# A fused polysketch attention and squared-ReLU layer: weights kept as loaded, one-run queries, padded tail keys, squares on GpSimd

## The chip, the cores and the metric

The kernel runs on one core of one Trainium2 chip. Its time is device time in microseconds (us) of one execution. The instructions belong to five engines: TensorE (PE in the profile, with its weight loads as PEld), VectorE (DVE), ScalarE (ACT), GpSimd (POOL) and SyncE (SP), which only issues transfers here. Each engine works through its own instructions in the order in which the program holds them; between engines, semaphores make one wait for another. A profile is one execution on the chip as the hardware recorded it.

## The reference

Inputs are `q`, `k`, `v` of 4 batches, 4 heads, 1088 tokens and 32 elements, two sketches `S1` and `S2` of 8x32, and the weights of a feed-forward layer. All are float32.

```python
def phi(x):                                   # 32 -> 64 features
    a = np.einsum('rd,bhsd->bhsr', S1, x)
    b = np.einsum('rd,bhsd->bhsr', S2, x)
    return np.einsum('bhsi,bhsj->bhsij', a, b).reshape(*x.shape[:-1], r * r)
q_p, k_p = (phi(q), phi(k))
kv = np.einsum('bhsf,bhsd->bhfd', k_p, v)
z = np.sum(k_p, axis=2)
num = np.einsum('bhsf,bhfd->bhsd', q_p, kv)
den = np.einsum('bhsf,bhf->bhs', q_p, z)[..., None] + 1e-06
x = (num / den)                               # -> 4352 tokens x 128
h = x @ w_in                                  # w_in 128 x 2048
g = np.maximum(h, 0.0) ** 2
out = g @ w_out                               # w_out 2048 x 128
```

## The kernel before

The attention is done batch by batch in float32. For the keys of a batch, `keys` turns `k` with 32x32 transposes on DVE (`kT`), multiplies by the sketches on PE (`kpr`, line 484), turns the result into `kab` (line 496), and forms the outer products `kp` (line 118, on POOL for most). 1088 tokens over 128 partitions give 8 full columns `l` = 0 to 7 and a ninth, `l` = 8, that fills only 64 partitions. `gram` (`z`, line 350) sums products of the sketched keys for the denominator, and `kvsum` (`kv`, line 365) multiplies `kp` by `v`; both have 64-partition matmuls for the ninth column. `kv_out` copies the sum out (`KVT`), turns it (`rep`) and copies it again (`KVr`).

For the queries of a batch, `queries` turns `q`, multiplies it by sketch and denominator weights, and brings that into `ab`. Batch 0 has a path of its own. Batch 1 does it with eight matmuls in two pieces (line 708) that ACT copies out. Batches 2 and 3 use small 32x32 tiles of the PE array: two pieces, each with eight matmuls for two of the four heads (line 728), and each transposed into `ab` by DVE (line 736). Then come the division (`tm`, `dn`, `rc`, `am`), the outer product `qp`, its transpose `tp`, and the multiplication by `KVr` (`x`, lines 592 and 622), whose result is copied out as bf16 (`xe`).

The feed-forward layer, `chunk`, takes 512 tokens at a time in eight chunks, and a ninth of 256 tokens (chunk 8, the tail tokens of all batches). A chunk has groups of 1024 columns of hidden values. `f1` (line 803) makes them in two PSUM banks with two matmuls of 512 columns, `re` is the ReLU out of PSUM (on ACT, line 812, or DVE, line 814), `sq` the square (on DVE, line 819, or ACT, line 821), and `f2` (line 827) multiplies by `w_out` with eight matmuls of 128 columns. `r` and `g` have four buffers each, the hidden values two pairs of banks for most groups. `oe` copies a chunk's output out of PSUM and `st` stores it.

`w_in` is cast to bf16 by `cast_w` (`cwi`) in four parts. In memory a part's hidden columns lie as `c`, `u` with `u` = 0 to 3 the fastest; the cast reads them with a step of four and writes each `u` together.

What runs when isn't decided at run time: `define` only records operations, and the string `ORDER` lists them by name, with `@ENGINE` where an operation can run on several. The instructions of each engine follow that list. Operations named `wm` are matmuls on zeros that fill PE's time in the first part. `BANKS` gives the PSUM bank of each value. The numbers beside an operation in `define` (such as `0.432`) were used to make the list and do nothing in the kernel.

Of the kernel before, what the change touches and what calls it, by code (L numbers as in the profile page):

```python
# [10 lines left out]
F32 = mybir.dt.float32  # L11
# [28 lines left out]
FILLS = 46  # L40


def define(W, tc, sb, ps, q, k, v, S1, S2, moe_w_in, moe_w_out, out):
# [12 lines left out]
    v_rest = sb.tile([64, B, H, D], F32, name="v_rest")  # L56
# [24 lines left out]
    w_in_b = sb.tile([128, CT, 128], BF16, name="w_in_b")  # L81
# [198 lines left out]
    def cast_w(i):  # L280
        @op("ACT", f"cwi{i}", act(512), r=[f"w_in_f{i}"], w=[f"w_in{i}"], alt=[("DVE", dve(512), 0)])
        def _(e):
            copy(
                e, w_in_b[:, 4 * i : 4 * i + 4], w_in_f[:, 512 * i : 512 * (i + 1)].rearrange("p (c u) -> p u c", u=4))

    def cast_wo(i):
        @op("ACT", f"cwo{i}", act(512), r=[f"w_out_f{i}"], w=[f"w_out{i}"], alt=[("DVE", dve(512), 0)])
        def _(e):
            copy(e, w_out_b[:, 4 * i : 4 * i + 4], w_out_f[:, 4 * i : 4 * i + 4])
# [51 lines left out]
    def gram(b, part):  # L341
# [4 lines left out]
        @op("PE", f"z{b}_{part}", 0.06 if part == 0 else 0.31, r=[f"kab{i}_{l}" for l in ls], w=[f"z{b}"], ps=[f"KZ{b}"])  # L346
        def _():
            for l in ls:
                x, pp = l % 4, 128 if l < NL else 64
                nc.tensor.matmul(  # L350
                    bank(f"KZ{b}")[32 * x : 32 * x + 32, 64:96],
                    kab[i][:pp, 1, l].rearrange("p h r -> p (h r)"), kab[i][:pp, 0, l].rearrange("p h r -> p (h r)"),
                    start=(l < 4), stop=(l + 4 > NL), skip_group_check=True)

    def kvsum(b, l0, n, last):
        i = b % 2
        r = [f"kp{i}_{l}" for l in range(l0, l0 + n)]
        r += [f"v_in{b}c{c}" for c in range(4)] if l0 < NL else [f"v_rest{b}"]

        @op("PE", f"kv{b}_{l0}", 0.10 * n, r=r, w=[f"kvt{b}"], ps=[f"KZ{b}"], after=[f"z{b}_0"])  # L360
        def _():
            for l in range(l0, l0 + n):
                pp = 128 if l < NL else 64
                for h in range(H):
# [3 lines left out]
                        kp[i][:pp, l, h].rearrange("p x y -> p (x y)"),  # L368
# [89 lines left out]
    def keys(b):  # L458
# [12 lines left out]
        else:  # L471
            spans = [(0, 4), (4, 4)] if b == 0 else [(0, 8)]
            for l0, n in spans:
# [3 lines left out]
                @op("PE", f"kpr{b}_{l0}", 0.28 if n == 4 else 0.63,  # L477
# [101 lines left out]
    def x_of(b, nm, l0, n, src, tn, pr, kind, rest=False):  # L579
# [4 lines left out]
        for f in range(2):  # L584
            @op("PE", f"{val}_{f}", 0.14 if n == 4 else 0.16, ps=[val],
# [25 lines left out]
    def x_whole(b, src, tn):  # L611
# [5 lines left out]
        @op("PE", f"x{b}", 1.43, ps=vals, r=[f"{tn}_{l}" for l in range(NL)] + [f"KVr{b}"], w=vals)  # L617
# [77 lines left out]
    def queries(b):  # L695
# [22 lines left out]
        else:  # L718
            for pr in range(2):
                val = f"qq{b}_{pr}"  # L720
                W.value(val, 2, "m")

                @op("PE", f"qpr{b}_{pr}", 0.59, r=[f"qT{i}_0", f"qT{i}_1", "Wqc", "Wqpad", f"Wqz{b}"], w=[val], ps=[val])
                def _(pr=pr, val=val):
                    for c in range(4):
                        for e in range(2):
                            h = 2 * pr + e
                            nc.tensor.matmul(  # L728
                                bank(val, e)[32 * c : 32 * c + 32, :256],
                                Wq[32 * h : 32 * h + 32, b].rearrange("p a r -> p (a r)"),  # L730
                                qT[i][32 * h : 32 * h + 32, :, c, :], start=True, stop=True, skip_group_check=True)
# [49 lines left out]
    def chunk(ci):  # L781
        rest = ci == 8
        ng = 4 if rest else 8
        W.value(f"o{ci}", 1, "o")
# [7 lines left out]
        nu = 1024 // N  # L792
        for g in range(ng):
            n = sum(8 for _ in range(ci)) + g
            hv = f"h{ci}_{g}"
            W.value(hv, 2, "h")

            @op("PE", f"f1_{ci}_{g}", 0.432, r=xk + [f"w_in{(nu * g + nu - 1) // 4}"], w=[hv], ps=[hv])
            def _(g=g, hv=hv):
                p0 = W.bank_of[hv]  # L800
                hh = P[:, p0 : p0 + 2].rearrange("p b n -> p (b n)")
                for u in range(nu):
                    nc.tensor.matmul(  # L803
# [204 lines left out]
```

## Time and profile before

| | |
|---|---|
| time, median of 3 runs | 107.2 us (106.2 to 108.21) |
| time of the profiled execution | 106.24 us |
| its span | 104.5 us |
| PE busy | 97.6 us, 93% of the span |
| DVE busy | 88.3 us, 85% |
| ACT busy | 87.4 us, 84% |
| POOL busy | 36.8 us, 35% |

The span is the part of the execution that the profile covers; 1.74 us of the profiled time lie around it. The profiled execution is at the fast end of the runs shown. The lines of one engine overlap a little at their ends, so that a run of eight instructions lasts less than eight times one of them; where the prediction needs the pace of an operation, it takes it from such a run.

### The profile page before, as it was taken

What the parts mean: (1) busy time and instruction counts of PE and PEld (TensorE: products, weight loads), DVE (VectorE), ACT (ScalarE), POOL (GpSimd) and SP (SyncE); (2) the same over time, 40 slices, a digit from 0 to 9 for tenths busy, and PEclk for the clock granted to TensorE, in tenths of its full rate; (3) what the DMA queues carried; (4) which work ended last, traced back from release to release, by engine and by line L of the source; (5) the groups of instructions that cost most, each with busy time, mean ns of one, the idle gap of its engine ahead of it and who ended that gap; (6) DMA issues with size and microseconds to landing.
All of it is one profiled execution on the core that took longest, in us unless ns stands there. A gap on an engine that the chain in (4) does not pass through costs nothing.

```text
span 104.5 us, 4039 instructions
## 1 busy us (share of the span) xinstructions
PE 97.6 (93%) x1716; PEld 68.1 (65%) x1716; DVE 88.3 (85%) x169; ACT 87.4 (84%) x105; POOL 36.8 (35%) x58
## 2 busy tenths in 40 slices
PE   5979999899899999999999999999999999999930
PEld 4757785377766665476777647677857677669930
DVE  2076898699799999999999999999998799999800
ACT  3104856999999999999999999999978999998910
POOL 3039436394049890026999700900000000000000
PEclk9999999999999999999999999999999999999996
DMA  2999999999998000000000300232000002510341
GB/s 80 340 252 309 296 281 396 316 202 242 292 189 171 30 9 0 6 0 0 0 9 10 122 0 6 69 86 102 0 6 0 0 0 60 137 38 9 98 112 42
DMA packets 7911, 11.28 MB, mean 108 GB/s; under 512 B 2261, under 2 KB 4949, under 8 KB 7893
## 3 DMA queue, kind: packets, MB, share of 16 engines
q1 hardware_dynamic: 7764, 10.98, 39.5%
q8 instruction: 13, 0.21, 1.0%
q10 hardware_dynamic: 128, 0.04, 0.2%
q14 instruction: 6, 0.04, 0.1%
HBM read 8.79 MB, written 2.23 MB: 105 GB/s over the span
## 4 chain that ended last, share of the span: by engine, by line
PE 83%; ACT 6%; DMA 4%; issue 2%; DVE 1%
PE P L827 30%; PE P L803 28%; PE P L365 5%; DMA k_in<-in_k_dram 4%; PE P L622 4%; ACT r L812 4%; PE P L728 2%; PE P L592 2%; PE P L196 2%; PE P L665 2%; PE P L484 2%; PE P L350 1%; PE P L381 1%; ACT w_in_b L115 1%; PE P L708 1%
## 5 line engine op out<-in xcount | busy, mean ns | idle before, releaser
L812 ACT ACTIVATE r<-P 128x1024 bf16<-128x1024 f32 x59 | 57.2, 1061 | 1.7 <-PE P L803 0.7
L827 PEld LDWEIGHTS <-g 128*128 128x128 bf16 x544 | 34.1, 98 | 11.7 <-ACT g L821 0.8
L827 PE MATMUL P<-w_out_b,g 128*128 128x128 bf16 x544 | 39.3, 219 | 0.0
L803 PE MATMUL P<-xT,w_in_b 128*128 128x512 bf16 x128 | 37.3, 379 | 0.6 <-ACT r L812 0.6
L819 DVE TENSOR_TENSOR g<-r 128x1024 bf16<-128x1024 bf16 x47 | 30.7, 682 | 2.5 <-PE P L827 1.4
L821 ACT ACTIVATE g<-r 128x1024 bf16<-128x1024 bf16 x21 | 21.8, 1108 | 0.0
L118 POOL TENSOR_TENSOR kp<-kab 128x512 f32<-128x512 f32 (+2 forms) x19 | 16.8, 907 | 2.0 <-DVE kab L496 2.0
L803 PEld LDWEIGHTS <-w_in_b 128*128 128x128 bf16 x144 | 11.8, 99 | 4.8 <-issue 2.8
L118 POOL TENSOR_TENSOR qp<-ab 128x512 f32<-128x512 f32 (+1 forms) x14 | 13.0, 945 | 1.8 <-DVE ab L118 1.5
L814 DVE TENSOR_SCALAR r<-P 128x1024 bf16<-128x1024 f32 x9 | 10.6, 1211 | 0.3 <-ACT r L812 0.2
L575 DVE STREAM_TRANSPOSE qpT<-qp 128x1024 f32<-128x1024 f32 (+2 forms) x12 | 10.1, 862 | 0.1
L196 PE MATMUL P<-zeros 128*128 128x256 bf16 x46 | 7.7, 313 | 1.1 <-DVE zeros L193 1.1
L297 DVE STREAM_TRANSPOSE kT<-k_in 128x512 f32<-128x512 f32 x8 | 5.3, 677 | 3.3 <-DMA k_in<-in_k_dram 3.3
L118 POOL TENSOR_TENSOR ab<-ab,rec 128x256 f32<-128x256 f32 (+1 forms) x4 | 2.3, 572 | 11.9 <-DVE rec L546 11.9
L196 PEld LDWEIGHTS <-zeros 128*128 128x128 bf16 x46 | 4.6, 112 | 2.8 <-DVE zeros L193 1.0
L118 POOL TENSOR_TENSOR tmp<-ab 128x256 f32<-128x256 f32 x2 | 1.8, 923 | 9.7 <-DVE ab L736 5.5
L365 PE MATMUL P<-kp,v_in 128*32 128x64 f32 x256 | 4.8, 221 | 0.0
L365 PEld LDWEIGHTS P<-kp,v_in 128*32 128x32 f32 x256 | 3.8, 110 | 1.4 <-issue 0.6
L115 DVE COPY osb<-P 128x512 f32<-128x512 f32 x7 | 4.7, 670 | 0.0
L622 PE MATMUL P<-qpT,KVr 32*32 32x256 f32 x192 | 4.5, 385 | 0.0
L496 DVE STREAM_TRANSPOSE kab<-P 128x512 f32<-128x512 f32 (+1 forms) x5 | 2.8, 583 | 1.9 <-PE P L484 1.9
L297 DVE STREAM_TRANSPOSE qT<-q_in 128x512 f32<-128x512 f32 x6 | 4.1, 682 | 0.0
(91 smaller groups left out, 87.8 us busy)
## 6 DMA issues: line engine op xcount, KB each, us to landing
k_in<-in_k_dram SPq DMA_DIRECT2D x4, 544.0 KB, 6.0
v_in<-in_v_dram SPq DMA_DIRECT2D x16, 128.0 KB, 6.4
q_in<-in_q_dram SPq DMA_DIRECT2D x3, 544.0 KB, 7.7
out_dram<-osb SPq DMA_DIRECT2D x24, 64.0 KB, 1.7
w_in_f<-in_moe_w_in_dram SPq DMA_DIRECT2D x4, 256.0 KB, 5.9
w_out_f<-in_moe_w_out_dram SPq DMA_DIRECT2D x4, 256.0 KB, 6.2
q_in<-in_q_dram SPq DMA_DIRECT2D x1, 512.0 KB, 6.0
out_dram<-osb SPq DMA_DIRECT2D x2, 256.0 KB, 3.4
```

The lines of the kernel that those rows point to most:

```text
L118: (nc.gpsimd if e == "POOL" else nc.vector).tensor_tensor(op=ALU.mult, **kw)
L196: W.op("PE", name, 0.107, lambda: nc.tensor.matmul(P[:, 3, :256], zeros[:, :128], zeros, start=True, stop=True, skip_group_check=True), r= ...
L297: nc.vector.transpose(dst[:, l0 : l0 + 4], src[:, :32].rearrange("p (c l) d -> p l c d", c=4)[:, l0 : l0 + 4])
L365: nc.tensor.matmul(bank(f"KZ{b}")[32 * h : 32 * h + 32, 0:64], v_in[b][:, h, l, :] if l < NL else v_rest[:, b, h, :], kp[i][:pp, l, h].rea ...
L575: nc.vector.transpose(dst[:, l0 : l0 + n].rearrange("p l h f t -> p (l h f t)"), src[:, l0 : l0 + n].rearrange("p l h x y -> p (l h x y)"))
L622: nc.tensor.matmul(bank(vals[c // 2], c % 2)[32 * h : 32 * h + 32, :256], KVr[b][32 * c : 32 * c + 32, f, 32 * h : 32 * h + 32], src[32 * ...
L803: nc.tensor.matmul(hh[:, N * u : N * (u + 1)], w_in_b[:, nu * g + u, :], x(), start=True, stop=True, skip_group_check=True)
L812: nc.scalar.activation(rt[n % NR], h, ACTF.Relu)
L814: nc.vector.tensor_scalar_max(rt[n % NR], h, 0.0)
L819: nc.vector.tensor_mul(gt[n % NG], rt[n % NR], rt[n % NR])
L821: nc.scalar.activation(gt[n % NG], rt[n % NR], ACTF.Square)
L827: nc.tensor.matmul(bank(f"o{ci}")[:, 128 * m : 128 * m + 128], gt[n % NG][:, N * u + 128 * m : N * u + 128 * m + 128], w_out_b[:, nu * g + ...
```

## The change

Parts of the code:

- `w_in_b` keeps the order of memory. The cast reads and writes without a step, and the weight load of `f1` reads 128 columns with a step of four elements.
- The queries of batch 1 go the way of batches 2 and 3. For these three batches one piece `qpr` of 16 matmuls for all four heads takes the place of two of eight, and DVE transposes its two halves into `ab`. `Wq` and its padding are as before.
- The ninth column of the keys is padded to 128 partitions: `pads` writes zeros once, and `gram` and `kvsum` use 128 partitions for all nine.
- A square may run on POOL.
- In chunk 8 the last group of 1024 columns becomes two groups of 512, each with one bank. Its output lies in two banks, copied out by ACT and DVE at once. Two of the four stores of chunk 7 are issued by ACT's queue.
- There are six fills fewer, and a new list `ORDER` with new `BANKS`. ReLUs: 59 on ACT and 9 on DVE before, 50 and 19 now. Squares: 21 on ACT and 47 on DVE before, 24 and 35 now, and 10 on POOL. `kv` is split into more separate pieces between the feed-forward matmuls: for batches 1, 2 and 3 it was 3, 1 and 1 pieces, and is 5, 3 and 2.

```diff
-    v_rest = sb.tile([64, B, H, D], F32, name="v_rest")
+    v_rest = sb.tile([128, B, H, D], F32, name="v_rest")
...
-    w_in_b = sb.tile([128, CT, 128], BF16, name="w_in_b")
+    w_in_b = sb.tile([128, 4, 128, 4], BF16, name="w_in_b")
...
+    @op("DVE", "pads", 1.1, w=["pads"])
+    def _():
+        nc.vector.memset(v_rest[64:], 0.0)
+        for i in range(2):
+            nc.vector.memset(kab[i][64:, :, NL], 0.0)
+            nc.vector.memset(kp[i][64:, NL], 0.0)
...
         def _(e):
-            copy(
-                e, w_in_b[:, 4 * i : 4 * i + 4], w_in_f[:, 512 * i : 512 * (i + 1)].rearrange("p (c u) -> p u c", u=4))
+            copy(e, w_in_b[:, i].rearrange("p c u -> p (c u)"), w_in_f[:, 512 * i : 512 * (i + 1)])
...
             for l in ls:
-                x, pp = l % 4, 128 if l < NL else 64
+                x = l % 4
                 nc.tensor.matmul(
                     bank(f"KZ{b}")[32 * x : 32 * x + 32, 64:96],
-                    kab[i][:pp, 1, l].rearrange("p h r -> p (h r)"), kab[i][:pp, 0, l].rearrange("p h r -> p (h r)"),
+                    kab[i][:, 1, l].rearrange("p h r -> p (h r)"), kab[i][:, 0, l].rearrange("p h r -> p (h r)"),
...
                         v_in[b][:, h, l, :] if l < NL else v_rest[:, b, h, :],
-                        kp[i][:pp, l, h].rearrange("p x y -> p (x y)"),
+                        kp[i][:, l, h].rearrange("p x y -> p (x y)"),
...
+            if b in QW:
+                vals = [f"qq{b}_{pr}" for pr in range(2)]
...
+                @op("PE", f"qpr{b}", 0.57, r=[f"qT{i}_0", f"qT{i}_1", "Wqc", "Wqpad", f"Wqz{b}"], w=vals, ps=vals)
+                def _(vals=vals):
+                    for c in range(4):
+                        for h in range(H):
+                            nc.tensor.matmul(
+                                bank(vals[h // 2], h % 2)[32 * c : 32 * c + 32, :256],
+                                Wq[32 * h : 32 * h + 32, b].rearrange("p a r -> p (a r)"),
+                                qT[i][32 * h : 32 * h + 32, :, c, :], start=True, stop=True, skip_group_check=True)
...
+        groups = [(0, 4), (4, 4), (8, 4), (12, 2), (14, 2)] if rest else [(2 * g, 2) for g in range(8)]
+        for g, (u0, nu) in enumerate(groups):
...
                     nc.tensor.matmul(
-                        hh[:, N * u : N * (u + 1)], w_in_b[:, nu * g + u, :], x(), start=True, stop=True,
+                        hidden()[:, N * u : N * (u + 1)], w_in_b[:, v // 4, :, v % 4], x(), start=True, stop=True,
...
-                if e == "DVE":
-                    nc.vector.tensor_mul(gt[n % NG], rt[n % NR], rt[n % NR])
+                r_, g_ = rt[n % NR][:, :cols], gt[n % NG][:, :cols]
+                if e != "ACT":
+                    product(e, out=g_, in0=r_, in1=r_)
...
+        if rest:
+            for m, e0 in enumerate(("ACT", "DVE")):
+                @op(e0, f"oe_{ci}{m}", act(128) if m == 0 else dve(128), r=[ov[m]], w=[f"osb{oi}_{m}"], ps=[ov[m]])
+                def _(m=m, e0=e0):
+                    copy(e0, osb[oi][:, m], o_of(m))
...
+                eng = "ACT" if ci == 7 and c > 1 else "SP"
...
-    TMK, TMQ, XW = (), (1,), (1, 2, 3)
+    TMK, TMQ, XW, QW = (), (), (1, 2, 3), (1, 2, 3)
...
-kp1_0@POOL kp1_6@POOL kp1_2@POOL kp1_4@POOL kp1_8@POOL f1_0_3 re_0_3@DVE x04_1_0 x04_0_0 x04_0_1
+tp0qp06 kab1_0 re_0_1@ACT sq_0_0@POOL kp1_8@POOL Wqc f1_0_2 f1_0_3 x04_1_0 x04_1_1 z1_0 z1_1
```

Three places show what the new list does. The first is POOL, from the end of batch 0 to the queries of batch 1. The tile `kp1` holds the key products of batch 1, `kp0` those of batches 0 and 2; `g0` to `g3` and `r0` to `r3` are the buffers of the feed-forward layer. Before:

```order
L118 TENSOR_TENSOR qp0_90<-ab0_87 128x256 x2
L252 TENSOR_TENSOR Wqf_145<-STS_136,maskh_139 128x4x16
L118 TENSOR_TENSOR kp1_86<-kab1_84 128x512 x4
L118 TENSOR_TENSOR kp1_86<-kab1_84 64x256
L118 TENSOR_TENSOR tmp1_97<-ab1_88 128x32x8
L118 TENSOR_TENSOR ab1_88<-ab1_88,rec1_103 128x32x8
L118 TENSOR_TENSOR qp1_91<-ab1_88 128x512 x4
```

The same place of the changed kernel:

```order
L118 TENSOR_TENSOR qp0_90<-ab0_87 128x256 x2
L118 TENSOR_TENSOR g0_124<-r0_120 128x1024
L118 TENSOR_TENSOR kp1_86<-kab1_84 64x256
L266 COPY Wq_144<-STS_136 128x4x16
L118 TENSOR_TENSOR kp1_86<-kab1_84 128x512 x4
L118 TENSOR_TENSOR g0_124<-r0_120 128x1024
L118 TENSOR_TENSOR g3_127<-r3_123 128x1024
L118 TENSOR_TENSOR ab1_88<-ab1_88,rec1_103 128x32x8
L118 TENSOR_TENSOR qp1_91<-ab1_88 128x512 x2
```

Three squares (`sq_0_0`, `sq_0_4`, `sq_0_7`) now stand around the key products of batch 1, and a product of the division (`tmp1`) has gone to DVE.

The second is DVE in chunk 0. `r` written from `P` is a ReLU, `g` from `r` a square, `qT1` and `kT0` are turned inputs of batches 1 and 2. Before:

```order
L819 TENSOR_TENSOR g2_126<-r2_122 128x1024
L819 TENSOR_TENSOR g3_127<-r3_123 128x1024
L425 TENSOR_REDUCE Wq_144<-P_63 128x8
L115 CAST w_out_b_134<-w_out_f_132 128x512
L819 TENSOR_TENSOR g0_124<-r0_120 128x1024
L819 TENSOR_TENSOR g1_125<-r1_121 128x1024
L819 TENSOR_TENSOR g2_126<-r2_122 128x1024
```

The changed kernel, in the same chunk:

```order
L848 TENSOR_SCALAR r3_123<-P_63 128x1024
L118 TENSOR_TENSOR g1_125<-r1_121 128x1024
L398 TENSOR_TENSOR Gm1_112<-P_63,maskg_141 128x32
L848 TENSOR_SCALAR r0_120<-P_63 128x1024
L848 TENSOR_SCALAR r1_121<-P_63 128x1024
L303 STREAM_TRANSPOSE qT1_81<-q_in1_69 128x512
L431 TENSOR_REDUCE Wq_144<-P_63 128x8
L303 STREAM_TRANSPOSE qT1_81<-q_in1_69 128x512
L848 TENSOR_SCALAR r3_123<-P_63 128x1024
L757 STREAM_TRANSPOSE ab1_88<-P_63 128x2x8x32 x2
```

In chunk 0 DVE has mostly ReLUs now and a single square, and the two transposes of batch 1's queries, which ACT copied before.

The third is the end of ACT's list; `osb1` is the output of chunk 7, `osb2` that of chunk 8. Before:

```order
L812 ACTIVATE r2_122<-P_63 128x1024
L812 ACTIVATE r3_123<-P_63 128x1024
L115 COPY osb1_129<-P_63 128x512
L115 COPY osb2_130<-P_63 128x256
L844 DMA out_0_dram<-osb2_130 32x256
```

The end of ACT's list in the changed kernel:

```order
L846 ACTIVATE r2_122<-P_63 128x1024
L846 ACTIVATE r3_123<-P_63 128x512
L115 COPY osb1_129<-P_63 128x512
L902 DMA out_0_dram<-osb1_129 32x512 x2
L115 COPY osb2_130<-P_63 128x128
L887 DMA out_0_dram<-osb2_130 32x256
```

The last ReLU and the last copy are half as wide, and two stores of chunk 7 are issued between the two copies.

More of the change, by code (lines that the diff above doesn't have):

```diff
@@ L357, in kvsum @@
         r = [f"kp{i}_{l}" for l in range(l0, l0 + n)]
-        r += [f"v_in{b}c{c}" for c in range(4)] if l0 < NL else [f"v_rest{b}"]
-        @op("PE", f"kv{b}_{l0}", 0.10 * n, r=r, w=[f"kvt{b}"], ps=[f"KZ{b}"], after=[f"z{b}_0"])
+        r += [f"v_in{b}c{c}" for c in range(4)] if l0 < NL else [f"v_rest{b}", "pads"]
+        @op("PE", f"kv{b}_{l0}", 0.112 * n, r=r, w=[f"kvt{b}"], ps=[f"KZ{b}"], after=[f"z{b}_0"])
         def _():
             for l in range(l0, l0 + n):
-                pp = 128 if l < NL else 64
                 for h in range(H):
@@ L825, in _ @@
+            @op("PE", f"f2_{ci}_{g}", 0.22 if half else 0.44, r=[f"g{n % NG}", f"w_out{wk}"], w=ov, ps=ov)
+            def _(n=n, u0=u0, nu=nu):
                 for u in range(nu):
@@ L936 @@
[L936 to L940 removed]
+warm0 ident LS1 LS2 sel wm0 wm1 wm2 wm3 wm4 wm5 wm6 wm7 wm8 wm9 wm10 wm11 wm12 wm13 wm14 wm15 wm16
```

225 lines of the change are left out of this document (118 added, 107 removed).

## The prediction

> **What bounds the kernel now.** I read the page's head and chain first, then the engines' busy time by stretches, then the chain in order of time and the engines' timelines where a term needs a duration.
>
> ```profile
> span 104.5 us, 4039 instructions
> PE 97.6 (93%) x1716; PEld 68.1 (65%) x1716; DVE 88.3 (85%) x169; ACT 87.4 (84%) x105; POOL 36.8 (35%) x58
> ...
> PE 83%; ACT 6%; DMA 4%; issue 2%; DVE 1%
> ```
>
> ```profile
> 22.00:97.00 75.00, 74.68 (x1302) 51.72 (x1294) 72.04 (x128) 73.32 (x83) 26.25 (x29) 1.00 0.25 60
> 52.00:62.00 10.00, 10.00 (x239) 6.74 (x236) 9.87 (x18) 9.89 (x11) 7.45 (x8) 1.00 0.11 37
> 76.00:86.00 10.00, 10.00 (x174) 6.78 (x173) 8.98 (x17) 8.89 (x11) 0.00 (x0) 1.00 0.01 2
> ```
>
> The second view's columns are the stretch, its length, then busy time of PE, PEld, DVE, ACT and POOL, and the granted clock. From 22 to 97 us PE is idle for 0.3 us. In the middle DVE and ACT have 0.1 us of slack in 10, and in 76 to 86 us 1.0 and 1.1. So PE bounds the kernel, and the two engines that feed it are almost as full. A saving on PE is worth its full length only where the feeders get lighter too. The clock is granted in full, so no term comes from it.
>
> **The change, part by part.** The sum is over PE's path, against the profiled execution's own 106.24 us (span 104.5 us and 1.74 around it).
>
> Queries. The chain in order of time (start, length, what) has the old pieces, the pieces of `f1` and `f2` that follow them, and such pieces with nothing before them:
>
> ```profile
> 24.65 0.92 PE P L708 x8
> ...
> 40.63 0.59 PE P L728 x16
> 41.22 0.55 PE P L827 x8
> ...
> 42.93 0.54 PE P L803 x2
> 43.47 0.45 PE P L827 x8
> 43.91 0.43 PE P L803 x2
> ...
> 76.26 1.43 PE P L622 x62
> ```
>
> A float32 matmul shows as two instructions. Batch 1 has two pieces of 0.92 us. Batches 2 and 3 have two of 0.59 us each, and the feed-forward piece behind each takes 0.55 or 0.54 instead of 0.45 or 0.43 us: 0.1 us for going back from small tiles. The new piece is 16 matmuls of 256 columns on 32x32 tiles, four row strips in turn. L622 has 32 such matmuls in the same turn in 1.43 us, so half of it, 0.72 us, and 0.1 behind. Batch 1: 1.84 to 0.82. Batches 2 and 3: 1.38 to 0.82 each. That is -1.02 - 2 x 0.56 = -2.1 us. If the four strips double the rate, the new piece takes 0.59 (-2.5 us); if they give nothing, 1.18 (-0.8). I take L622, whose tiles are the same.
>
> Padding. PE's own timeline over keys and `gram` of batch 2 and 3:
>
> ```profile
> 52.50 1.10 PE L365 MATMUL P<-kp,v_in 128*32 128x64 f32 x64
> 53.53 0.32 PE L365 MATMUL P<-kp,v_rest 64*32 64x64 f32 x8
> 53.77 0.51 PE L350 MATMUL P<-kab 128*32 128x32 f32 x18
> 54.21 0.62 PE L827 MATMUL P<-w_out_b,g 128*128 128x128 bf16 x8
> ```
>
> By the starts, 64 instructions take 1.03 us, 16 ns each, but the eight of 64 rows 0.24 and the 18 of `gram`, of which two have 64 rows, 0.44. At 16 ns they would be 0.13 and 0.29: -0.11 and -0.15 us, in four batches -1.0 us. If only the eight gain it is -0.4. The zeros of `pads` are written by DVE ahead of its first key transpose, which waits for the load of `k` anyway; without that cover they would cost about 1 us.
>
> More pieces. `kv` is cut into five more pieces and `x04` into one more. Each has small tiles between feed-forward matmuls, so 0.1 us by the rows above: +0.6 us. A second switch at the piece's own start would double it, so up to +1.2.
>
> Start. The chain from the first copies of `x`:
>
> ```profile
> 16.86 0.37 ACT xT L115
> 17.23 1.02 ACT w_in_b L115
> 18.26 2.76 ACT r L812 x3
> ```
>
> The cast with the step stands between `x` and the first ReLU on ACT. Now a cast of `w_out` stands there, and the other goes to DVE. These rows have the durations:
>
> ```profile
> L115 ACT CAST w_in_b<-w_in_f 128x512 bf16<-128x512 f32 x3 | 3.4, 1144 | 0.0
> L115 ACT CAST w_out_b<-w_out_f 128x512 bf16<-128x512 f32 x2 | 1.3, 644 | 0.0
> ```
>
> So the first ReLU comes 1144 - 644 = 0.5 us earlier: -0.5 us. It is nothing if the matmuls come later than that, -1.0 if the whole cast goes.
>
> The feeders. These rows give the pace of their operations, and what POOL takes by size:
>
> ```profile
> 40.55 7.65 ACT L812 ACTIVATE r<-P 128x1024 bf16<-128x1024 f32 x8
> 48.04 4.87 ACT L821 ACTIVATE g<-r 128x1024 bf16<-128x1024 bf16 x5
> 42.04 1.85 DVE L819 TENSOR_TENSOR g<-r 128x1024 bf16<-128x1024 bf16 x3
> 48.42 3.49 DVE L814 TENSOR_SCALAR r<-P 128x1024 bf16<-128x1024 f32 x3 [0.17 <-ACT r L812]
> L115 DVE COPY osb<-P 128x512 f32<-128x512 f32 x7 | 4.7, 670 | 0.0
> L118 POOL TENSOR_TENSOR kp<-kab 128x512 f32<-128x512 f32 x12 | 12.7, 1074 | 2.0 <-DVE kab L496 2.0
> L118 POOL TENSOR_TENSOR kp<-kab 128x256 f32<-128x256 f32 x3 | 1.9, 620 | 0.0
> ```
>
> A ReLU is 0.96 us on ACT and 1.16 on DVE, a square 0.97 and 0.62. ACT: nine ReLUs fewer (one half as wide) is -9.0, three squares more +2.9, three casts without the step -1.5 us, less some 3 us for copies that it takes over: -4 to -5 us. DVE: ten ReLUs more (one half) +11.0, twelve squares fewer (two of the rest half) -8.1, two transposes for batch 1 at no more than 0.7 each +1.3, and eleven copies, casts and products that go to ACT or POOL at 0.4 to 0.7 each, about -5.7: -1.5 us. Both get lighter, DVE by less than PE. A square on POOL isn't in the trace: going on from 620 and 1074 ns by the same step it is 2.0 us. It could be 1.1 if bf16 went twice as fast, as on DVE, or 2.15 at twice the wider row. I take 2.0; ten are 20 us on an engine that is busy for 36.8.
>
> Pace of the ReLUs. Late in the kernel, where ACT has nearly all ReLUs, it sets PE's pace:
>
> ```profile
> 78.71 15.91 ACT L812 ACTIVATE r<-P 128x1024 bf16<-128x1024 f32 x17 [0.43 <-PE P L803]
> ```
>
> ```profile
> 90.21 0.47 PE P L803 x2
> ```
>
> `f1` takes 0.47 there instead of 0.43, in about nine groups. Now DVE has two of these ReLUs and POOL a square: -0.3 us (0 to -0.35).
>
> Tail. The end of the chain, and SP's last transfers:
>
> ```profile
> 100.27 0.37 ACT osb L115
> ```
>
> ```profile
> 100.67 0.32 SPq L841 DMA_DIRECT2D out_dram<-osb  x1
> 101.03 0.42 SPq L856 DMA_DIRECT2D out_dram<-osb  x1
> ```
>
> The last copy gets half as wide (about 0.1 less), and no store is left behind the last one on SP (0.36 between the starts): -0.4 us. ACT issues two stores ahead of its last copy; at 0.42 each, and with the copy of chunk 7 (0.67 by DVE's row), they are done in 1.5 us. PE needs four `f2` of 0.45, or 1.8 us, from the end of chunk 7 to that copy, so they are hidden. If not, the gain is gone.
>
> New waits. PE comes to some groups earlier than the feeders do. In chunk 0 and 1 the banks of two `f1` now wait for ReLUs at the end of a row of DVE instructions (the second place in the section on the change). Behind a waiting `f1` stand PE's whole list, and behind it ACT. I take +0.8 us, two waits of a ReLU's third; none is possible, and 3.5 would be three whole ReLUs.
>
> Sum: -2.1 - 1.0 + 0.6 - 0.5 - 0.3 - 0.4 + 0.8 = -2.9 us. The profiled execution would take 103.3 us. The median of the runs shown, 107.2, lies 0.96 above it, so I expect a median of **104.3 us**.
>
> [...]
>
> ```profile
> 26.42 0.41 DVE L115 CAST w_out_b<-w_out_f 128x512 bf16<-128x512 f32 x1
> 29.38 0.95 DVE L115 CAST w_out_b<-w_out_f 128x512 bf16<-128x512 f32 x1
> ```
>
> ```profile
> 28.93 1.11 POOL L118 TENSOR_TENSOR tmp<-ab 128x256 f32<-128x256 f32 x1 [4.22 <-ACT ab L115]
> 44.60 0.73 POOL L118 TENSOR_TENSOR tmp<-ab 128x256 f32<-128x256 f32 x1 [5.52 <-DVE ab L736]
> ```
>
> The same cast takes 0.41 us with POOL idle and 0.95 with POOL's product running until 30.04, after which 0.29 is left. POOL's product itself took 1.11 instead of 0.73. So they hold each other up. [...]
>
> [...]
>
> **The rivals.**
>
> 1. The feeders eat the gain. Of the 75 us from 22 to 97 (first stretch above) DVE was idle for 3.0; it gets 1.5 lighter and has to be 2.9 faster. That leaves 1.6 us. If DVE is held up or late by 3 to 5 us, 1.4 to 3.4 of it shows: 105.7 to 107.7 us. For it: the shares of DVE. Against: ReLUs out of PSUM and transposes, which have one input, ran beside POOL without a loss (10 us with 7.45 of POOL above).
>
> 2. Slower: POOL's squares stand in the way of DVE's. If each of the ten holds one DVE instruction for half its 2.0 us, DVE loses 10 us, of which 8.4 is beyond its slack: 104.3 + 8.4 = 112.7 us. It decides from 1.6 us and makes the kernel slower from about 4.5 us. For it: the cast above. Against: the three squares at the first place stand beside a stretch in which DVE has ReLUs and transposes.
>
> 3. Slower: the strided weight load.
>
> ```profile
> L803 PEld LDWEIGHTS <-w_in_b 128*128 128x128 bf16 x144 | 11.8, 99 | 4.8 <-issue 2.8 <-DVE xT L115 0.2 <-ACT w_in_b L115 0.2
> L708 PEld LDWEIGHTS P<-Wqf,qT 128*128 128x128 f32 x16 | 2.0, 192 | 0.1
> ```
>
> A load takes 99 ns for 256 bytes of a partition and 192 for 512, so it may go by the bytes that it passes. With the step these are 1024: about 390 ns, where a matmul of 512 columns gives 0.43 / 2 = 215 ns of cover. It decides from 215 ns; at 390 the 128 matmuls cost 22 us more and the 16 narrower ones of chunk 8 5 us: 131 us. At 192 all is hidden but in chunk 8, whose matmuls take half of 215: 16 x 84 ns is +1.3 us, inside the range.
>
> 4. The change doesn't save PE time: four strips give nothing (-0.8 instead of -2.1) and `gram` gains nothing (-0.4 instead of -1.0). Then it is -1.0 us: 106.2 us.
>
> **How the numbers follow.** Forecast 0.58, giving 101.6 (all terms near their good ends: -2.5 - 1.4 + 0.6 - 1.0 - 0.3 - 0.5 is -5.1 us, and half a microsecond of waits) to 105. Rivals 1 and 4 together 0.28, the milder form of rival 2 among them: 105 to 107.7. Rival 2 in full 0.06, rival 3 in full 0.05, other mishaps 0.01. About 2% (2.1 us) is what a measurement can tell from no change: faster is below 105.1, slower above 109.3. So 0.60 faster (some of rival 1 falls there), 0.28 within, 0.12 slower. The range that holds 8 in 10 is 101.6 to 107.7 us.
>
> **What would show it.** The piece of 16 matmuls with line 734 lasts about 0.7 us on PE. The eight of `kv` for the ninth column take 0.13 us by the starts. The first ReLU stands in the chain near 17.8 us instead of 18.26. POOL's squares last 2.0 us. If the prediction is wrong by rival 1, PE shows waits for DVE of some microseconds in chunks 0 to 4; by rival 2, DVE's squares last 1 us or more where POOL has one; by rival 3, pieces of `f1` last well over 0.43 us. If waits are none, the time is below 103.5.

## The result and the profile after

The changed kernel is slower. Its median is 111.59 us (111.41 to 113.94, four runs) beside 107.01 us (106.2 to 108.21, four runs): a ratio of 1.045, with a 95% interval of 1.037 to 1.053. The forecast was 104.3 us with a range up to 107.7, so sign and range were both wrong: the change was expected to gain 2.7% and loses 4.5. The profiled execution took 111.61 us. Some executions of either kernel are disturbed and take some per cent longer (113.94 us here; 110.6 beside 105.76 for the kernel before), so all ratios are between undisturbed ones, and from the profiled executions of e1, e5, e9 and e13, which were disturbed, little more is read than which instruction overlaps which, and for how long.

The page of the changed kernel, head, busy time, clock and the shares of the chain:

```profile
span 109.8 us, 4053 instructions
...
PE 96.5 (88%) x1704; PEld 68.6 (62%) x1726; DVE 93.6 (85%) x161; ACT 84.3 (77%) x106; POOL 59.0 (54%) x72
...
PEclk9999999999769999999999999999999999999999
...
PE 62%; DVE 18%; issue 10%; DMA 4%; ACT 1%; POOL 1%; DVEq 0%; POOLq 0%
```

PE's share of the chain has fallen from 83 to 62%, and two slices near 30 us have a lower clock, which before only the last slice had. Busy time by stretches (length, PE, PEld, DVE, ACT, POOL, granted clock) puts a place to it:

```profile
22.00:32.00 10.00, 6.55 (x112) 3.91 (x113) 9.29 (x8) 6.11 (x10) 5.74 (x5) 0.83 1.08 243
```

From 22 to 32 us PE works for 6.55 us, but DVE seems busy for 9.29, with eight instructions. The timelines of DVE, POOL and PE there (start, length, what; in brackets the idle time before and who ended it):

```profile
20.67 1.23 DVE L848 TENSOR_SCALAR r<-P 128x1024 bf16<-128x1024 f32 x1 [0.30 <-PE P L838]
21.81 4.58 DVE L118 TENSOR_TENSOR g<-r 128x1024 bf16<-128x1024 bf16 x1
26.31 0.18 DVE L398 TENSOR_TENSOR Gm<-P,maskg 128x32 f32<-128x32 f32 x1
...
21.50 0.23 POOL L266 COPY Wq<-STS 128x64 f32<-128x64 f32 x1
21.69 4.15 POOL L118 TENSOR_TENSOR kp<-kab 128x512 f32<-128x512 f32 x4
...
23.50 0.62 PE L863 MATMUL P<-w_out_b,g 128*128 128x128 bf16 x8
26.45 0.62 PE L863 MATMUL P<-w_out_b,g 128*128 128x128 bf16 x8 [2.33 <-DVE g L118]
27.68 0.38 PE L838 MATMUL P<-xT,w_in_b 128*128 128x512 bf16 x1 [0.61 <-DVE r L848]
28.81 1.01 PE L838 MATMUL P<-xT,w_in_b 128*128 128x512 bf16 x2 [0.40 <-DVE r L848]
31.19 1.06 PE L734 MATMUL P<-qT,Wq 32*32 32x256 f32 x32
```

This is the whole case. One square on DVE, `sq_0_1`, lasts 4.58 us where others last 0.68. It starts 0.12 us after the first of POOL's four key products of batch 1, and ends 0.55 us, about one square's own length, after the fourth ends at 25.84. The `f2` that reads it waits 2.33 us; the two ReLUs behind it on DVE are late too, and the `f1` groups that need their banks wait 0.61 and 0.40 us.

In the kernel before, POOL works through the same key products, but DVE's first square starts 0.40 us after the last of them has ended (19.96 and 4.75 is 24.71):

```profile
19.96 4.75 POOL L118 TENSOR_TENSOR kp<-kab 128x512 f32<-128x512 f32 x5 [1.63 <-DVE kab L496]
...
25.11 1.28 DVE L819 TENSOR_TENSOR g<-r 128x1024 bf16<-128x1024 bf16 x2
```

A held instruction counts as busy here. In the chain of waits, the hold appears as time without a cause, "issue":

```profile
21.89 0.71 DVE g L118
22.60 3.71 issue
26.31 0.17 DVE Gm L398
26.48 1.07 issue
27.55 1.22 DVE r L848
```

A second, shorter hold is that of `sq_1_5`, beside two products of batch 2:

```profile
44.71 2.16 DVE L118 TENSOR_TENSOR g<-r 128x1024 bf16<-128x1024 bf16 x1
...
44.67 1.65 POOL L118 TENSOR_TENSOR kp<-kab 64x256 f32<-64x256 f32 x2
```

PE stops twice shortly behind it, for 0.21 us (an `f2` that waits for DVE's `g`) and 0.64 us (key matmuls that wait for a copy on DVE).

The groups show what the forecast was afraid of (squares on POOL, weight loads with a step) and the mean of DVE's squares, which was 682 ns before (the first row is of the kernel before):

```profile
L819 DVE TENSOR_TENSOR g<-r 128x1024 bf16<-128x1024 bf16 x47 | 30.7, 682 | 2.5 <-PE P L827 1.4
...
L118 DVE TENSOR_TENSOR g<-r 128x1024 bf16<-128x1024 bf16 x33 | 27.0, 854 | 0.5 <-ACT r L846 0.4
...
L118 POOL TENSOR_TENSOR g<-r 128x1024 bf16<-128x1024 bf16 x10 | 19.4, 1941 | 20.3 <-ACT r L846 11.7 <-PE P L863 5.9 <-DVE r L848 2.4
...
L838 PEld LDWEIGHTS <-w_in_b 128*128 128x128 bf16 x144 | 13.6, 115 | 7.1 <-issue 5.2
```

### The profile page after: what moved, and what is told of

Its sections match the earlier page's. It is cut to its first block, busy times and chain, and to the rows that moved or that the text cites. A ratio compares the mean times of both kernels' runs of the same rounds, so it can differ in the third digit from the quotient of the medians.

```text
span 109.8 us, 4053 instructions
## 1 busy us (share of the span) xinstructions
PE 96.5 (88%) x1704; PEld 68.6 (62%) x1726; DVE 93.6 (85%) x161; ACT 84.3 (77%) x106; POOL 59.0 (54%) x72
## 4 chain that ended last, share of the span: by engine, by line
PE 62%; DVE 18%; issue 10%; DMA 4%; ACT 1%; POOL 1%; DVEq 0%; POOLq 0%
PE P L863 24%; PE P L838 20%; DVE r L848 6%; DMA k_in<-in_k_dram 4%; PE P L371 3%; PE P L598 3%; DVE g L118 3%; PE P L628 3%; PE P L734 2%; DVE qpT L581 2%; PE P L490 2%; DVE osb L115 1%; DVE kT L303 1%; DVE ab L757 1%; DVE den L548 1%
## 5 line engine op out<-in xcount | busy, mean ns | idle before, releaser
L846 ACT ACTIVATE r<-P 128x1024 bf16<-128x1024 f32 (+1 forms) x50 | 47.8, 1018 | 7.8 <-remote 3.6
L838 PE MATMUL P<-xT,w_in_b 128*128 128x512 bf16 x106 | 34.0, 385 | 2.6 <-DVE r L848 1.5
L118 POOL TENSOR_TENSOR g<-r 128x1024 bf16<-128x1024 bf16 x10 | 19.4, 1941 | 20.3 <-ACT r L846 11.7
L118 DVE TENSOR_TENSOR g<-r 128x1024 bf16<-128x1024 bf16 (+1 forms) x35 | 27.7, 829 | 0.5 <-ACT r L846 0.4
L857 ACT ACTIVATE g<-r 128x1024 bf16<-128x1024 bf16 x24 | 24.6, 1060 | 1.1 <-PE P L863 1.0
L848 DVE TENSOR_SCALAR r<-P 128x1024 bf16<-128x1024 f32 (+1 forms) x19 | 22.4, 1188 | 3.4 <-PE P L838 2.3
L838 PEld LDWEIGHTS <-w_in_b 128*128 128x128 bf16 x144 | 13.6, 115 | 7.1 <-issue 5.2
L118 POOL TENSOR_TENSOR qp<-ab 128x512 f32<-128x512 f32 (+1 forms) x16 | 15.0, 958 | 2.4 <-DVE ab L118 2.1
L757 DVE STREAM_TRANSPOSE ab<-P 128x512 f32<-128x512 f32 x6 | 3.9, 696 | 1.2 <-PE P L734 1.2
L115 ACT CAST xT<-P 128x256 bf16<-128x256 f32 (+1 forms) x6 | 2.5, 444 | 2.1 <-PE P L598 2.0
```

The costliest lines, as they stand in the source:

```text
L118: (nc.gpsimd if e == "POOL" else nc.vector).tensor_tensor(op=ALU.mult, **kw)
L757: nc.vector.transpose(ab[i][:, :, 2 * pr : 2 * pr + 2].rearrange("p l h a r -> p h l (a r)"), P[:, p0 : p0 + 2, :256].rearrange("p h (l t) ...
L838: nc.tensor.matmul(hidden()[:, N * u : N * (u + 1)], w_in_b[:, v // 4, :, v % 4], x(), start=True, stop=True, skip_group_check=True)
L846: nc.scalar.activation(rt[n % NR][:, :cols], hidden(), ACTF.Relu)
L848: nc.vector.tensor_scalar_max(rt[n % NR][:, :cols], hidden(), 0.0)
L857: nc.scalar.activation(g_, r_, ACTF.Square)
```

## The experiments

Theory T: the loss is one event. A DVE square comes 0.12 us too late and is kept out by a row of POOL products (4.58 us instead of 0.68), PE stops for it (2.33 us), and then runs for a while at a lower clock (0.83 as the mean of 22 to 32 us). Against it stand A (POOL's ten squares hold DVE up all over the kernel), B (DVE has too many ReLUs) and C (the strided weight load or other new code).

### e1 and e2: the held squares go to ACT

```diff
-... cwi2@ACT xex04_1_4@ACT ... cwi3@ACT sq_0_1@DVE Gm1 ...
+... cwi2@ACT sq_0_1@ACT xex04_1_4@ACT ... cwi3@ACT Gm1 ...
```

> One square (sq_0_1, 1024 columns) goes from DVE to ACT; all else as in the changed kernel. Theory T (this one DVE square waits out four key products that stand back to back on POOL, 4.58 us instead of 0.62, and PE stands still for it and then runs at a lower clock): PE's stop of 2.33 us before the second f2 of chunk 0 goes, the granted clock from 22 to 32 us is above 0.95, median 106 to 108 us. Rival A (POOL's ten squares hold DVE up all over the kernel): one square matters little, 110.5 to 111.5 us. Rival B (DVE has too many ReLUs): about 111 us, since DVE's queue only loses 0.6 us of work. Rival C (strided weight load or other new code): 111.5 us.

Ratio to the kernel before: 1.002 (0.997 to 1.008). One square on another engine brings the 4.5% back. The stretch of the stop now reads

```profile
22.00:32.00 10.00, 8.30 (x187) 5.24 (x188) 8.72 (x14) 9.18 (x14) 6.79 (x6) 1.00 1.09 222
```

with the full clock. A, B and C are out as causes of the loss. But T's range went down to parity and below, and the forecast gain doesn't come back with it; that is taken up from e7 on.

e2 moves `sq_1_5` to ACT as well.

```diff
-sq_1_4@ACT sq_1_6@ACT ... kTr3 sq_1_5@DVE dn2ab00
+sq_1_4@ACT sq_1_5@ACT sq_1_6@ACT ... kTr3 dn2ab00
```

> As the first, and sq_1_5 (2.16 us on DVE beside POOL's products of batch 2) goes to ACT too. Theory T: another 0.5 to 1.5 us, so 105 to 107 us. If only the first stop counts, the same as the first kernel within 0.5 us. Rivals A to C: 110 to 111.5 us.

It took 106.74 and 106.83 us in two executions, beside 106.31 to 106.96 for e1 on the same chip: nothing is gained. In its trace PE's stops of 0.21 and 0.64 us are gone, but two of 0.77 and 0.11 us stand in their place, for copies of `x` that ACT now does behind the square. So the move gains nothing; that the second hold itself costs nothing isn't shown.

### e3: POOL's order alone

```diff
-kp1_6@POOL kp1_4@POOL kp1_0@POOL kp1_2@POOL kv1_0 sq_0_4@POOL
+sq_0_4@POOL kp1_6@POOL kp1_4@POOL kp1_0@POOL kp1_2@POOL kv1_0
```

> POOL's list alone is changed: its square of group 4 stands ahead of the four key products of batch 1 instead of behind them. It needs a ReLU that DVE does after sq_0_1, so the products can't start beside sq_0_1. Theory T: sq_0_1 takes about 0.65 us again and PE's stop of 2.33 us goes, but the products end some 4 us later and the kv pieces of batch 1 wait for them: 108 to 110.5 us. If the square was long for another reason than the products beside it, it stays at 4 us or more and the time at 111 us or above.

The ratio is 1.048 (1.040 to 1.057), 111.33 us: above the expected range, though the square is short again.

```profile
22.12 0.68 DVE L118 TENSOR_TENSOR g<-r 128x1024 bf16<-128x1024 bf16 x1
...
29.54 0.43 PE L371 MATMUL P<-kp,v_in 128*32 128x64 f32 x16 [3.14 <-POOL kp L118]
```

The square takes 0.68 us without the products beside it, but the products end later, and PE stops for them for 3.14 us instead. The granted clock falls here too, to 0.50 from 30.17 to 33.58 us. T was right on the square and wrong on the price: the wait only changed its name.

### e5: half a microsecond more work on POOL

Three fills of an unused tile, 0.72 us by the trace, stand ahead of the four products, so that the square starts first.

```diff
-kp1_6@POOL kp1_4@POOL kp1_0@POOL kp1_2@POOL
+idle kp1_6@POOL kp1_4@POOL kp1_0@POOL kp1_2@POOL
```

> The changed kernel with three more instructions on POOL, some 0.5 us of filling an unused tile, ahead of the four key products of batch 1, so that sq_0_1 starts on DVE just before the first product instead of 0.12 us behind it. Theory T (whoever comes first keeps the other out, and POOL's row of products let DVE in only behind the fourth): the square takes 0.62 to 0.75 us, PE's stop of 2.33 us and the window at half clock go, and the kernel with more work is 4 to 5 us faster: 106 to 107.5 us. If the square is long for another reason, or simply because DVE is overloaded: 111.5 to 112 us.

Ratio 0.998 (0.992 to 1.005): the kernel with more work is 4.7% of the kernel before faster than the same kernel without it. DVE and POOL at that place:

```profile
26.57 0.66 DVE L118 TENSOR_TENSOR g<-r 128x1024 bf16<-128x1024 bf16 x1
...
25.91 0.72 POOL L215 MEMSET idle<- 128x128 f32 x3
26.59 2.59 POOL L118 TENSOR_TENSOR kp<-kab 128x512 f32<-128x512 f32 x2
```

The square comes 0.02 us ahead of the first product and takes 0.66 us; now the product waits for it (two take 2.59 instead of about 2.1). Nothing else in the kernel differs. This shows that the order of two starts decides.

### e4: all ten squares of POOL go to DVE

```diff
-sq_0_0@POOL ... sq_0_4@POOL ... sq_6_5@POOL
+sq_0_0@DVE ... sq_0_4@DVE ... sq_6_5@DVE
```

> All ten squares of POOL go to DVE, at the same places of the order. Rival A (POOL's squares are what holds DVE up): the loss goes, 105 to 107.5 us. Theory T: the four key products still stand beside sq_0_1, now from about 20.4 to 24.5 us, so it is still held for some 3 us; DVE has 10 x 0.62 = 6.2 us more to do: 110 to 113 us.

Ratio 1.099 (1.085 to 1.112), 117.04 us: 4 us above T's range. POOL's squares aren't the harm; they take some 6 us off DVE (ten at 0.62). What they left behind shows in batch 3, where four squares stand beside POOL's products:

```profile
48.75 2.90 DVE L118 TENSOR_TENSOR g<-r 128x1024 bf16<-128x1024 bf16 x2
...
48.56 6.52 POOL L118 TENSOR_TENSOR kp<-kab 128x512 f32<-128x512 f32 x5
```

Here the two engines take turns: a square takes about 1.45 us, and the five products 6.52 instead of about 5.2. `sq_0_1` took 1.46 us in this kernel, beside the same four products, where T had expected a hold of some 3 us.

### e15 and e9: when does DVE get in

e15 makes only the first of these ten moves.

```diff
-re_0_1@ACT sq_0_0@POOL kp1_8@POOL
+re_0_1@ACT sq_0_0@DVE kp1_8@POOL
```

> The changed kernel with its first square (sq_0_0) on DVE instead of POOL, all other squares where they were. POOL's four products then start some 1.9 us earlier, beside sq_0_0. If DVE gets in after one product once POOL has had to wait for DVE itself (as where all ten squares were moved): sq_0_1 takes 1.3 to 1.6 us, PE's stop is 1 us or less, 107 to 109 us. If a row of products always keeps DVE out to its end: sq_0_1 takes 2.5 to 4 us and the time is 109.5 to 111 us.

Ratio 1.005 (1.000 to 1.010). DVE and POOL:

```profile
20.53 0.64 DVE L118 TENSOR_TENSOR g<-r 128x1024 bf16<-128x1024 bf16 x1
21.10 1.20 DVE L848 TENSOR_SCALAR r<-P 128x1024 bf16<-128x1024 f32 x1
22.23 1.45 DVE L118 TENSOR_TENSOR g<-r 128x1024 bf16<-128x1024 bf16 x1
...
20.68 4.96 POOL L118 TENSOR_TENSOR kp<-kab 128x512 f32<-128x512 f32 x4
```

The first product had to wait for `sq_0_0`. After that `sq_0_1`, which again came behind a product's start, got in after one product instead of four: 1.45 us. The time came out at the low end of the expected range.

e9 leaves the squares alone and puts one fill between the first and the second product.

```diff
-kp1_6@POOL kp1_4@POOL
+kp1_6@POOL idle kp1_4@POOL
```

> The changed kernel with one more instruction on POOL, a fill of an unused tile (some 0.2 us), between the first and the second of the four key products. The square on DVE still comes behind the first product. If POOL's row of products keeps DVE out because the next one is already there when one ends, the fill lets DVE in after the first: the square takes 1.4 to 1.8 us instead of 4.58, and the time is 107.5 to 109.5 us. If DVE is kept out until POOL's list stands still, whatever stands in it: 4.7 us and 111.5 us or more.

Ratio 1.043 (1.033 to 1.052): no help.

```profile
26.35 4.22 DVE L118 TENSOR_TENSOR g<-r 128x1024 bf16<-128x1024 bf16 x1
...
25.73 1.06 POOL L118 TENSOR_TENSOR kp<-kab 128x512 f32<-128x512 f32 x1
26.73 0.20 POOL L214 MEMSET idle<- 128x128 f32 x1
26.90 3.12 POOL L118 TENSOR_TENSOR kp<-kab 128x512 f32<-128x512 f32 x3
```

The square came in the middle of the first product and was kept out past the fill and three more. So a fill between two products doesn't let DVE in. What does isn't shown: in e15 and in most of e4 the POOL instruction just ahead had itself waited for DVE, but e4 also has two squares, of 1.14 and 1.19 us beside two `qp` products each, that got in after one product without that.

### e6: PE is kept busy while it waits

26 matmuls on zeros stand ahead of the `f2` and the `f1` that wait. They write into a PSUM bank that holds part of `x` for chunk 1, whose values are lost.

```diff
-f2_0_0 f2_0_1 f1_0_6
+f2_0_0 wn0 ... wn19 f2_0_1 wn20 ... wn25 f1_0_6
```

> The changed kernel with 26 matmuls on zeros (about 0.1 us each) on PE where it waits for sq_0_1 and for the two ReLUs behind it; the wait itself stays. If the clock at half speed from 27.3 to 30.7 us comes from PE's standing still, it stays full now: half of 3.4 us, 1.7 us, comes back where PE is the bound, so 109.7 to 110.5 us. If the clock falls for another reason, or its fall costs nothing: 111.5 us or a little more.

The ratio is 1.037 (1.026 to 1.048), beside 1.045 (1.037 to 1.053). The expectation has the lower clock from 27.3 to 30.7 us; by the trace of the changed kernel it lies from 28.59 to 32.00 us. Stretches of the changed kernel ahead of that and there, and then of e6 (the number behind POOL's is the clock):

```profile
25.18:28.59 3.41, 1.30 (x11) 1.03 (x13) 3.41 (x4) 0.41 (x2) 1.48 (x2) 1.00 1.04 281
28.59:32.00 3.41, 3.19 (x58) 1.76 (x57) 2.70 (x5) 2.53 (x4) 1.07 (x1) 0.50 1.10 217
```

```profile
23.65 2.35 PE L196 MATMUL P<-zeros 128*128 128x256 bf16 x20
...
29.00:32.50 3.50, 3.50 (x100) 2.16 (x99) 3.47 (x7) 3.50 (x5) 0.34 (x1) 1.00 1.10 200
```

With the fills the clock stays full, so it fell because PE stood still. What that is worth, 0.9 us by the two ratios, is about a fifth of the loss, and the intervals overlap; the 1.7 us that I expected are not there.

### e7, e14 and e10: the queries

e7 is e1 with each batch's query piece written as two again, one behind the other.

```diff
-qpr1 kv1_2 ... qpr2 ... qpr3
+qpr1_0 qpr1_1 kv1_2 ... qpr2_0 qpr2_1 ... qpr3_0 qpr3_1
```

> The first experiment's kernel (sq_0_1 on ACT) with the queries of batches 1 to 3 in two pieces of 16 matmuls again (still three elements), at the same place of PE's list. The prediction has one piece of 0.72 us for two of 0.59: 3 x 0.46 = 1.4 us of PE time more than the first experiment, whose ratio to the kernel before was 1.002: 1.010 to 1.016. If the feeders bound chunks 0 to 2 and not PE: no more than 0.5 us, up to 1.007.

Ratio 0.994 (0.988 to 1.000), and for the same kernel once more as e14 on another chip 1.000 (0.994 to 1.005). It isn't slower than e1 but if anything faster, and my expectation missed. The two pieces still run as one (here in e14, 0.66 us from start to start):

```profile
26.39 0.73 PE L749 MATMUL P<-qT,Wq 32*32 32x256 f32 x32 [0.23 <-ACT r L846]
```

> The seventh experiment's kernel once more, beside e13 on one chip. Ratio 0.990 to 1.000 as before, with sq_1_5 at 0.66 us where DVE gets in ahead of POOL's products and 2.16 where it doesn't.

By luck of the timing `sq_1_5` also starts before POOL's products in e7 and e14 and takes 0.66 and 0.65 us, and PE's stops of 0.21 and 0.64 us behind it are gone. So that e7 is a little faster than e1 may come from there; what shows that the split costs nothing is the row above. e10 takes the pieces apart:

```diff
-qpr1_0 qpr1_1 kv1_2 ... f2_1_1 ... f2_3_5
+qpr1_0 kv1_2 qpr1_1 ... f2_1_1 qpr2_1 ... f2_3_5 qpr3_1
```

> The seventh experiment's kernel with the second piece of queries one piece of other work later in PE's list (a kv piece in batch 1, an f2 in batches 2 and 3), so that the two can't run at the same time. In the seventh, the two pieces side by side took 0.66 us together, as one piece does; before, each took 0.59. The prediction's working gives 0.59 + 0.59 - 0.66, and 0.1 for one more return from small tiles, 0.6 us in each of three batches: 1.8 us more than the seventh (0.9944), so about 1.011. If waits for the feeders take it up: 0.5 to 1 us, 0.999 to 1.004.

```profile
26.50 0.67 PE L749 MATMUL P<-qT,Wq 32*32 32x256 f32 x16 [0.23 <-ACT r L846]
27.09 0.43 PE L371 MATMUL P<-kp,v_in 128*32 128x64 f32 x16
27.45 0.66 PE L749 MATMUL P<-qT,Wq 32*32 32x256 f32 x16
```

By the starts each piece takes 0.59 us now, where both together took 0.66. In the three batches the pieces take 3.56 us by the starts, beside 1.95 in e14. The ratio is 1.015 (1.006 to 1.025), 1.6 to 2.1% above e14 and e7. Some 0.6 us of that may be another thing: `sq_1_5` is held again here, for 1.71 us, and PE stops for 0.11 and 0.48 us behind it. What is left is still over 1 us: the gain of the merged queries is real, and it comes from the two pieces standing side by side, not from the new loop.

### e8 and e11: two parts alone, in the kernel before

e8 has only the padded tail keys: the new `pads`, `gram` and `kvsum`, with `pads` behind `maskh` in the list.

```diff
-kab[i][:pp, 1, l] ... kab[i][:pp, 0, l] ... kp[i][:pp, l, h]
+kab[i][:, 1, l] ... kab[i][:, 0, l] ... kp[i][:, l, h]
```

> The kernel before with the padded tail keys alone. The prediction took -1.0 us (the eight matmuls of the ninth column from 0.24 to 0.13 us, gram from 0.44 to 0.29, in four batches), with -0.4 as the other end. The trace after showed gram at 0.38 and the ninth column still near 0.24: by that -0.2 to -0.4 us, ratio 0.996 to 0.999.

Ratio 0.9995 (0.995 to 1.004). PE's pieces do get shorter, in this batch by as much as the prediction had it:

```profile
53.95 0.30 PE L372 MATMUL P<-kp,v_rest 128*32 128x64 f32 x8
54.06 0.35 PE L358 MATMUL P<-kab 128*32 128x32 f32 x18
54.34 0.62 PE L834 MATMUL P<-w_out_b,g 128*128 128x128 bf16 x8
...
52.00:62.00 10.00, 9.81 (x243) 6.90 (x241) 10.00 (x18) 9.95 (x12) 7.97 (x9) 1.00 0.11 37
```

By the starts the eight take 0.11 us (0.24 before) and the 18 take 0.28 (0.44). But in that stretch DVE is busy for 10.00 of 10 us and ACT for 9.95: PE's saving becomes PE's waiting. My expectation, 0.996 to 0.999, lies just below the measured ratio, though inside its interval.

e11 has only `w_in_b` in loaded order, with its casts and its strided weight load.

```diff
-w_in_b[:, nu * g + u, :]
+w_in_b[:, v // 4, :, v % 4]
```

> The kernel before with w_in kept in loaded order alone: four casts without the step (1144 to about 640 ns on ACT), and 144 weight loads with a step of 8 bytes. The prediction took -0.5 us for the start and nothing for the loads: ratio about 0.995. If the loads were slow (third rival) 1.05 or more. If the first ReLU waits for something else than the cast: 0.999 to 1.001.

Ratio 0.999 (0.994 to 1.005).

```profile
L803 PEld LDWEIGHTS <-w_in_b 128*128 128x128 bf16 x144 | 13.3, 116 | 4.0 <-issue 2.5 <-DVE xT L115 0.2
...
17.33 0.62 ACT L115 CAST w_in_b<-w_in_f 128x512 bf16<-128x512 f32 x1
18.15 1.02 ACT L812 ACTIVATE r<-P 128x1024 bf16<-128x1024 f32 x1 [0.19 <-PE P L591]
```

A strided load takes 116 ns instead of 99 and is hidden. The cast is 0.5 us shorter, but the first ReLU starts at 18.15 as before, since there it waits for PE.

### e13 and e12: can the rest be had back

e13 gathers e14's `kv` matmuls into fewer pieces, on the same chip.

```diff
-kv1_0 qpr1_0 qpr1_1 kv1_2 ... kv1_4 f2_0_3 f1_1_1 kv1_6 f2_0_4 kv1_8 ... kv2_6 ... kv2_8 ... kv3_0 kv3_2 ... kv3_4
+qpr1_0 qpr1_1 kv1_0 kv1_2 ... f2_0_3 f1_1_1 f2_0_4 kv1_4 kv1_6 kv1_8 ... kv2_6 kv2_8 ... kv3_0 kv3_2 kv3_4
```

> The seventh experiment's kernel (sq_0_1 on ACT, queries in two neighbouring pieces) with PE's kv matmuls of batches 1 to 3 in four pieces instead of eight (later ones gathered behind one feed-forward piece). If the small pieces cost 0.14 us each in kv and some 0.1 us in the feed-forward piece behind: 0.6 to 1.0 us less than e14. If PE's waits for the feeders take it up: within 0.3 us of e14.

Ratio 1.012 (1.005 to 1.019) beside e14's 1.000: worse by 1.2%, against my expectation. The `kv` matmuls took 0.7 us less PE time by their starts; that waits took more than that is the likely account, but this profile is too rough to size them.

e12 is e2 with two casts of `w_out` and a copy of `x` moved from ACT to DVE.

```diff
-cwo2@ACT ... cwo3@ACT ... re_0_7@DVE ab1_0 ... xe1_0@ACT ... oe_0@DVE
+re_0_7@DVE cwo2@DVE cwo3@DVE ab1_0 ... xe1_0@DVE oe_0@DVE
```

> The second experiment's kernel (sq_0_1 and sq_1_5 on ACT) with two casts of w_out and one copy of x of batch 1 moved from ACT to DVE, at places where POOL stands still or DVE reads PSUM. By theory T what is left of the loss is waits for ACT between 18 and 43 us (0.3 to 0.8 us each), so 0.5 to 1.2 us less than the second experiment: 105.3 to 106.2 us, ratio 0.988 to 0.996. If PE's own work is the bound there, no gain: 1.000 to 1.004.

Ratio 1.010 (1.002 to 1.018): no gain either. No version that I ran is faster than the kernel before beyond its interval.

## Why the prediction was wrong

**The step that failed.** The prediction took "+0.8 us, two waits of a ReLU's third" for new waits, with 3.5 us as the other end, and it looked for them at banks and ReLUs. In its second rival it had the right mechanism, two engines that keep each other out, but put it at POOL's squares, "each of the ten" holding a DVE instruction, and gave 0.06, since "the three squares at the first place stand beside a stretch in which DVE has ReLUs and transposes". The order shown with the change says otherwise: between those ReLUs DVE has one square, and on POOL, between its squares, stand the four key products, which are old work. New was only that a square of DVE now stood beside them. The right question was not what the moved squares do, but which DVE square now meets which row on POOL, and what waits for it. Priced that way, four products of about 1.04 us are 4.15 us of hold, with PE's next `f2` behind it. So the term that failed is the +0.8 us of new waits: it had nothing in it for a DVE square beside POOL's products, and PE's stops behind that square alone are 2.33, 0.61 and 0.40 us, 3.3 us together.

**Who keeps whom out.** At these rows the one that starts first keeps the other out: in e5 the square starts 0.02 us ahead of the first product and takes 0.66 us, in the changed kernel 0.12 us behind it and takes 4.58. It can last longer than one instruction: in the changed kernel DVE was kept out for four products in a row, in e9 through a fill as well (4.22 us). The prediction's evidence was a cast of `w_out`, 0.95 us instead of 0.41 beside a single product; no row of the kernel before has a square beside a row of products. Not everything on DVE is held: a ReLU out of PSUM took 1.20 us beside e15's products, where the mean before was 1.21. The strided load, of which the prediction had no row either, took 116 ns instead of 99 (e11), and is hidden.

**Size of the loss.** By e1 the event costs 4.25% of the kernel before, about 4.5 us. The square is held for 3.9 us (4.58 less 0.68), which PE meets as the 3.3 us of stops; by e6 the clock adds some 0.9 us (the intervals overlap), and the rest isn't split up.

**The terms, in the repaired kernel.** Without the holds (e7, e14) the change is worth 0 to 0.6%, not 2.7%. The time from the first `f1` to the last `f2`, shared out by the starts of PE's matmuls (each from its start to the next one's, or to its own end where PE then stood idle), in us:

```
                                            before   e14
f2                                           31.51  32.09
f1                                           31.14  31.19
queries of batches 1 to 3                     4.32   1.95
x (qpT times KVr)                             5.25   5.47
kv, eight columns                             3.23   3.79
kv, ninth column                              0.74   0.62
gram                                          1.35   0.97
turning KV, Gm                                1.32   1.44
keys; tail tokens' queries and x              3.26   3.39
PE idle                                       0.80   1.96
sum                                          82.92  82.86
```

- Queries, forecast -2.1: -2.4. Right in size, and e10 finds it in the time.
- Padding, forecast -1.0 in four batches, so -0.75 in the three of this stretch: -0.5. `gram` gave what was forecast; the ninth column gave 0.04 us a batch instead of 0.11. In the kernel before, alone, no gain in time can be seen (e8).
- More pieces, forecast +0.6, at most 1.2: +0.6 in `kv`, +0.2 in `x`, +0.6 in `f2`, +0.25 in the rest, about +1.6. In `f2` it is the last matmul ahead of a piece of small tiles that takes longer, 0.149 us or more from start to start instead of 0.056; there are two such places before and eight in e14. That is the second switch, at the piece's own start, which the prediction named and left out of its sum. This is the term of the sum that was sized worst, apart from the hold.
- New waits, forecast +0.8: +1.2 without the holds. The two waits for ReLUs that I had in mind are there, 0.48 and 0.45 us.
- Start and tail, forecast -0.5 and -0.4: what lies outside the stretch went from 21.54 to 20.60 us, -0.9. That it agrees is luck. Behind the last `f2` it is 4.10 us instead of 4.23, so the tail gave 0.1. The other 0.8 us is the first `f1`, at 16.49 us instead of 17.31; but it stands at 17.35 in the changed kernel and at 17.58 in e15, whose lists are the same up to there, so this differs from execution to execution and no gain of the start is shown. In the changed kernel itself the first ReLU started at 17.98 instead of 18.15, and e11 shows that the cast alone does nothing.
- Pace of late ReLUs, forecast -0.3: `f1` is unchanged, 0.

**The rivals.** The first (feeders eat the gain) fits what is left once the squares are repaired: 1.2 us of waits, e8, e12 and e13. The second held in its mechanism, not in its place. The third (strided load) is refuted by e11, the fourth (no PE time saved) by the table and e10.

**What would show it.** The 0.7 us of the query piece, POOL's 2.0 us (1.94) and the load's cover were right. A ninth column of 0.13 us was seen in a batch of e8 (0.11), not on average. "By rival 2, DVE squares of 1 us or more where POOL has one" was nearly the right thing to look for: where POOL has a product. Two numbers of the working don't come out, though neither made the miss: 101.6 us is 106.24 less 4.6, without the 0.96 us that the forecast adds for the median, and the 1.4 us at the good end of the padding has no row behind it.

## What to carry to other kernels

When work moves between DVE and GpSimd, list for each DVE instruction of a kind that was held here (squares, 4.58 us instead of 0.68, and a cast of `w_out`, 0.95 instead of 0.41) what GpSimd has running at its start, and how many more products stand right behind that one; price the hold with the whole row, then follow who waits for the held engine. A PE saving is worth its length only where both feeders have slack in that stretch (in e8 DVE was busy for 10.00 of 10 us and ACT for 9.95, and the ratio was 0.9995), and gathering pieces can save work and lose time (in e13 0.7 us less PE time in `kv`, and 1.2% slower). Query pieces on different tiles of the PE array are worth placing next to each other, whichever loop writes them (0.66 us for both in e14, 0.59 for each apart in e10).

## What I had not expected of the hardware

- A DVE square was kept out for four GpSimd products in a row (4.58 us instead of 0.68), and 0.02 to 0.12 us of start time decide it (e5 and the changed kernel). In other places the engines took turns after one product (1.45 us). What decides between the two is open.
- The hold counts as DVE's busy time, and the chain calls most of it "issue". Here only the length of the single instruction, 4.58 us beside the usual 0.68, gives it away.
- After a stop of 2.33 us with two short ones behind it, TensorE's granted clock was 0.50 for 3.41 us. In the 3.41 us before, PE had 1.30 us of work. In e6, with filler matmuls in the stops, it was 1.00 from 22 to 32.5 us.
